# Windowed attention and a gated convolution on one core: the window as a band matmul ahead of the scores, and 25 of the loads of q and k by GpSimd's queue

## The chip, the cores and the metric

One core of a Trainium2 chip runs the whole program. TensorE (PE in the profile) multiplies matrices, VectorE (DVE), ScalarE (ACT) and GpSimd (POOL) work on elements, SyncE (SP) issues most of the DMAs. Each engine takes its own instructions strictly in the order of its own list; a semaphore wait holds the instruction that carries it and everything behind it on that engine. The metric is the device time of one execution in microseconds (us), the median over several runs.

## The reference, cut to what matters

Batch 8, 8 heads, 576 positions, 64 features to a head; then a feed-forward part with d_model 512 and d_ff 1024. Random fp32 inputs; the band, the convolution and the gate are:

```python
scores = scale * np.matmul(q, k.transpose(0, 1, 3, 2))
mask = np.abs(pos[:, None] - pos[None, :]) <= 32
scores = np.where(mask, scores, -1000000000.0)
...softmax over the keys...
x = np.matmul(attn, v)            # heads side by side: (batch, 576, 512)
h = np.maximum(x @ w_in, 0.0)
conv_out[s] = sum_k conv_w[k] * h[s - 1 + k]        # 3 taps, a weight for each of the 1024 features
out = (h * sigmoid(conv_out)) @ w_out
```

## The kernel before, in words

Everything is unrolled, and one text, `ORDER`, sets the order of the steps on all engines: each word is a step with its arguments, steps are issued in the order of the words, and every instruction is kept in that order on its engine. The digit behind an @ is the PSUM bank. A step whose data another engine or a DMA makes waits for it, and a step that reuses a buffer waits for the last reader of the buffer's old content; these waits follow from the order of the words.

Attention runs over units (b, G): a batch and a group of four heads. For each unit:

- `lq`, `lk` load 128 x 1152 fp32 of q or k (576 KB) into one of six staging tiles `st`, issued by SP; with a third argument after b and G they load half of it. `cq`, `ck` cast them to bf16 into one of the tiles `qb` (ending p: GpSimd, a: ScalarE). `tq`, `tk` transpose them on VectorE into `qT`, `kT`.
- `sc` computes the scores of four heads for one part of the positions (h = 0: four tiles of 64 queries, h = 1: five): per tile and half of the features, four matmuls with 32 rows of weights each, one for each head. `ex` takes the exponential on ScalarE into a tile `attn`. `mk` sets what lies outside the window to zero: on VectorE a product with a 0/1 tile `mask`, on GpSimd two affine selects.
- `lv` loads one of five chunks of v (192 or 256 KB) on SP, `cv` and `vo` cast and shift it (`ve`, `vo`), `av` multiplies with `attn`, `nr` divides by the row sums into `xn`; `xp` and `xe` transpose through TensorE and ScalarE, `xt` by a DMA.

The feed-forward part runs over pieces P (four halves of 192 columns, then ten of 384) and four pairs of feature blocks m2: `ph` multiplies by w_in (eight matmuls), `re` is the ReLU into `hT`, `pc` and `tp` are the three convolution taps, `th` the tanh, `ga` the gate into `gT`, `py` the product with w_out, `ye` and `st` copy and store the result. The taps have forms: P by six matmuls with 128 x 128 diagonal weights for a pair of blocks, D and A by twelve matmuls of 64 x 64, X by ScalarE and VectorE, G by GpSimd.

Weights are loaded and cast in four quarters each (`li`, `ci`, `lo`, `co`). While no data is there yet, TensorE runs products with the identity (`id,n`: n products of the identity itself; `ia,y,G,half,n`: n products that read the half of the cast tile `qb` of unit (0, G), y = 0 for q and 1 for k; nothing uses their results). A tile of `qb` is chosen by `slot(y, b, G) % NQB`, with `slot = 2 * (2 * b + G) + y`.

Of the kernel before, what the change touches and what calls it, by code (L numbers as in the profile page):

```python
# [13 lines left out]

ORDER = """
lk,0,0,0 lq,0,0,0 s3 s1 lq,0,0,1 lk,0,1,1 s2 lk,0,1,0 lk,0,0,1 cw@5 id,7@7 lq,0,1,1 lq,0,1,0 cc lv,0,2 dg,1,a dg,0,d
lv,0,1 dg,2,d cq,0,0,0,a ia,0,0,0,1@7 cq,0,0,1,p ia,0,0,1,2@7 dg,7,a ck,0,1,1,p ia,1,1,1,2@7 dg,4,a s4 tq,0,0,1 dg,5,a
tk,0,1,1 ck,0,0,0,p ia,1,0,0,6@7 dg,3,a s5 tq,0,0,0 s0 ck,0,1,0,a s7 tk,0,0,0 lv,0,3 ck,0,0,1,p ia,1,0,1,2@7 tk,0,0,1
cq,0,1,1,a tk,0,1,0 sc,0,0,1@4 tq,0,1,1 cq,0,1,0,p sc,0,0,0@0 ex,0,0,1 lv,0,4 tq,0,1,0 cv,0,2,p lv,0,0 ex,0,0,0
mk,0,0,1,d sc,0,1,1@4 id,4@3 lk,1,0 ex,0,1,1 cv,0,1,p li,1 vo,0,1,d li,3 sc,0,1,0@4 id,9@3 mk,0,0,0,d lq,1,0 cv,0,3,a  # L20
li,0 mk,0,1,1,d li,2 cv,0,4,a vo,0,2,d vo,0,3,d cv,0,0,a lq,1,1 ex,0,1,0 vo,0,0,d lk,1,1 av,0,0,0@0 mk,0,1,0,d lv,1,2
ck,1,0,a nr,0,0,0 av,0,1,0@3 id,1@7 nr,0,1,0 av,0,0,1@0 ci,1,a xp,0,1@6 nr,0,0,1 dg,6,a xp,0,0@2 xe,0,1,a ci,3,p
av,0,1,1@4 id,4@7 xe,0,0,a nr,0,1,1 ph,0,3@3 lv,1,1 cq,1,0,p tk,1,0 xp,0,2@7 re,0,3 xp,0,4@5 xp,0,3@4 xe,0,2,a
ph,0,1@0 xe,0,3,a tq,1,0 pc,0,3,P@6 ci,0,p re,0,1 ph,1,3@4 th,0,3,P xe,0,4,a ga,0,3,P sc,1,0,0@0 re,1,3 ph,0,0@5
ci,2,p ex,1,0,0 lv,1,0 pc,1,3,P@7 re,0,0 ph,2,0@4 mk,1,0,0,d th,1,3,P cq,1,1,p sc,1,0,1@0 ph,2,2@5 ex,1,0,1 ph,2,3@6
tq,1,1 re,2,2 ck,1,1,p lv,1,4 ph,2,1@3 ga,1,3,P ph,1,0@5 re,2,1 lv,1,3 tk,1,1 cv,1,2,p re,2,0 ph,1,1@0 re,1,0 re,1,1
mk,1,0,1,d lo,1 sc,1,1,0@1 cv,1,1,p lo,2 pc,0,1,P@5 ex,1,1,0 ph,0,2@7 cv,1,0,p vo,1,1,d re,2,3 sc,1,1,1@0 re,0,2
ph,1,2@4 vo,1,0,d ex,1,1,1 mk,1,1,0,d lv,2,1 av,1,0,0@6 lo,0 re,1,2 nr,1,0,0 cv,1,3,p av,1,1,0@0 lk,2,1 cv,1,4,a
pc,1,0,P@2 lo,3 nr,1,1,0 pc,1,2,P@4 vo,1,3,p th,1,0,P lv,2,0 pc,0,0,P@7 th,0,1,P ga,1,0,P th,1,2,P xp,1,0@3 mk,1,1,1,d
xp,1,1@6 co,1,p xe,1,0,a pc,1,1,P@1 lq,2,1 xe,1,1,a ga,1,2,P pc,0,2,P@2 lk,2,0 ga,0,1,P pc,2,0,X@0 ph,3,2@3 vo,1,2,p  # L30
th,1,1,P tp,2,0,X ph,3,0@4 re,3,2 th,0,2,P ph,3,1@6 re,3,0 lv,2,2 pc,3,2,G ga,0,2,P pc,2,3,P@5 th,0,0,P ga,1,1,P
re,3,1 av,1,0,1@3 co,0,a ga,0,0,P av,1,1,1@1 nr,1,0,1 pc,2,2,P@6 lq,2,0 co,2,a pc,2,1,P@7 ck,2,1,p nr,1,1,1 lv,2,3
ph,3,3@3 th,2,0,X th,2,3,P pc,3,0,P@4 re,3,3 co,3,p ga,2,3,P xp,1,4@1 th,2,1,P xp,1,3@2 pc,3,1,P@3 th,3,0,P ga,2,1,P
cv,2,0,p pc,3,3,P@5 xe,1,4,a ga,2,0,X th,2,2,P xp,1,2@1 cv,2,1,p th,3,1,P py,0,1@7 ga,2,2,P vo,2,0,p ga,3,1,P cq,2,1,a
s6 tk,2,1 lv,2,4 py,0,2@6 tp,3,2,G xe,1,2,a tq,2,1 th,3,3,P xe,1,3,a lq,3,0 ga,3,0,P lk,3,0 sc,2,1,0@0 ga,3,3,P
ck,2,0,p py,1,0@4 ex,2,1,0 ye,0,1,d cv,2,2,p th,3,2,G@5 lk,3,1 tk,2,0 ye,0,2,a vo,2,1,p sc,2,1,1@0 lv,3,0 cq,2,0,a
ga,3,2,G ph,4,3@6 ye,1,0,d ex,2,1,1 lv,3,1 tq,2,0 cv,2,3,p py,0,0@4 vo,2,2,p re,4,3 mk,2,1,0,d lk,4,0 cv,2,4,a
mk,2,1,1,d sc,2,0,1@0 ye,0,0,a vo,2,3,p av,2,1,0@6 ex,2,0,1 ph,4,2@4 nr,2,1,0 st,0,0 mk,2,0,1,d sc,2,0,0@0 cq,3,0,p
re,4,2 av,2,1,1@6 lq,3,1 st,0,1 ck,3,0,a nr,2,1,1 ph,4,1@4 pc,4,3,G ex,2,0,0 tk,3,0 av,2,0,1@6 re,4,1 ph,4,0@0
mk,2,0,0,d ck,3,1,a nr,2,0,1 av,2,0,0@4 re,4,0 pc,4,1,A@2 nr,2,0,0 xp,2,2@6 th,4,1,A pc,4,2,P@0 tq,3,0 tp,4,3,G  # L40
pc,4,0,P@4 th,4,2,P ga,4,1,A lv,3,2 py,1,2@7 xt,2,3 xt,2,1 th,4,0,P ga,4,2,P cv,3,0,a ga,4,0,P xe,2,2,a xt,2,0
sc,3,0,0@0 tk,3,1 cq,3,1,p py,1,1@6 th,4,3,G@4 st,0,2 ex,3,0,0 ga,4,3,G lq,4,0 st,1,0 cv,3,1,a mk,3,0,0,p sc,3,0,1@0
lq,4,1 ye,1,1,d py,2,0@4 lv,3,3 ex,3,0,1 tq,3,1 st,1,1 lv,3,4 ck,4,0,a mk,3,0,1,d sc,3,1,0@0 cv,3,2,p ph,5,2@5
ex,3,1,0 ye,1,2,d xt,2,4 vo,3,1,d ye,2,0,a sc,3,1,1@0 vo,3,0,d re,5,2 py,2,1@4 mk,3,1,0,d ex,3,1,1 pc,5,2,G tk,4,0
cq,4,0,a av,3,0,0@0 av,3,1,0@6 lq,5,0 ph,5,0@2 nr,3,0,0 cq,4,1,a nr,3,1,0 py,2,2@5 re,5,0 tq,4,0 xt,3,0 cv,3,3,a
ye,2,1,a mk,3,1,1,d vo,3,2,p sc,4,0,0@0 xt,3,1 ye,2,2,a pc,5,0,D@6 ex,4,0,0 ph,5,1@4 tq,4,1 lk,4,1 th,5,0,D cv,3,4,p
# [659 lines left out]
```

## Time and profile before

| | us |
|---|---|
| median of three runs | 212.5 (211.89 to 212.92) |
| the profiled execution, its own time | 212.45 |
| its span, first to last instruction | 210.7 |
| around the span | 1.75 |
| TensorE busy | 195.7 (93% of the span) |
| VectorE busy | 178.4 (85%) |
| ScalarE busy | 172.7 (82%) |
| GpSimd busy | 147.7 (70%) |
| 16 DMA engines, share of SP's queue | 84.0% |

The mean granted TensorE clock is 0.992 of full speed. Busy times overlap; what matters at any place is which engine or transfer is waited for there.

### The profile page before, as it was taken

What the parts mean: (1) busy time and instruction counts of PE and PEld (TensorE: products, weight loads), DVE (VectorE), ACT (ScalarE), POOL (GpSimd) and SP (SyncE); (2) the same over time, 40 slices, a digit from 0 to 9 for tenths busy, and PEclk for the clock granted to TensorE, in tenths of its full rate; (3) what the DMA queues carried; (4) which work ended last, traced back from release to release, by engine and by line L of the source; (5) the groups of instructions that cost most, each with busy time, mean ns of one, the idle gap of its engine ahead of it and who ended that gap; (6) DMA issues with size and microseconds to landing.
All of it is one profiled execution on the core that took longest, in us unless ns stands there. A gap on an engine that the chain in (4) does not pass through costs nothing.

```text
span 210.7 us, 7141 instructions
## 1 busy us (share of the span) xinstructions
PE 195.7 (93%) x2951; PEld 113.9 (54%) x2974; DVE 178.4 (85%) x297; ACT 172.7 (82%) x265; POOL 147.7 (70%) x177
## 2 busy tenths in 40 slices
PE   3867999999999799999999999999999999999994
PEld 2233798895465345654464554554545565555443
DVE  4677977999999998797999779899999587899860
ACT  2986798997999798779999699899978799759911
POOL 2650586499999469999699998539954879955700
PEclk9979999999999999999999999999999999999999
DMA  5999999999998895899999999999976444222225
GB/s 176 325 213 347 388 220 273 366 296 272 318 279 194 195 319 151 267 292 238 241 258 176 226 252 231 262 297 245 290 144 165 99 142 128 46 71 103 100 100 199
DMA packets 66165, 46.90 MB, mean 223 GB/s; under 512 B 53180, under 2 KB 55508, under 8 KB 66132
## 3 DMA queue, kind: packets, MB, share of 16 engines
q1 hardware_dynamic: 66096, 46.43, 84.0%
q8 instruction: 23, 0.38, 0.8%
q14 instruction: 10, 0.08, 0.1%
q10 hardware_dynamic: 36, 0.01, 0.1%
HBM read 32.52 MB, written 9.44 MB: 199 GB/s over the span
## 4 chain that ended last, share of the span: by engine, by line
PE 56%; DVE 16%; DMA 8%; SPq 7%; ACT 6%; issue 5%; ACTq 0%; DVEq 0%
PE PS L165 56%; SPq L165 7%; DVE gT L165 6%; DMA vst<-in_v_dram 6%; DVE xn L165 4%; DVE PS L165 2%; DMA st<-in_q_dram 2%; ACT hT L165 2%; ACT attn L165 1%; ACT PS L165 1%; DVE attn L165 1%; DVE rec L165 1%; ACT y L165 1%; DVE qT L165 1%; DVE kT L165 1%
## 5 line engine op out<-in xcount | busy, mean ns | idle before, releaser
L165 PE MATMUL PS<-xT,w_in_sb 128*128 128x385 bf16 (+3 forms) x448 | 69.5, 305 | 0.5 <-ACT y L165 0.3
L165 PE MATMUL PS<-w_out_sb,gT 128*128 128x512 bf16 (+1 forms) x273 | 64.7, 373 | 1.5 <-issue 0.5
L165 DVE SCALAR_TENSOR_TENSOR gT<-PS,hT 128x384 bf16<-128x384 f32 (+2 forms) x82 | 52.5, 649 | 3.9 <-ACT PS L165 2.9
L165 PEld LDWEIGHTS <-w_in_sb 128*128 128x128 bf16 x448 | 40.6, 98 | 23.1 <-issue 3.2
L165 ACT ACTIVATE hT<-PS 128x770 bf16<-128x770 f32 (+3 forms) x56 | 39.9, 722 | 9.7 <-PE PS L165 7.2
L165 PEld LDWEIGHTS <-gT 128*128 128x128 bf16 x296 | 27.6, 98 | 30.2 <-issue 1.2
L165 ACT ACTIVATE attn<-PS 128x1280 bf16<-128x1280 f32 (+1 forms) x32 | 36.0, 1132 | 4.9 <-PE PS L165 4.5
L165 POOL TENSOR_TENSOR zg<-zg,tap 128x768 f32<-128x768 f32 (+1 forms) x18 | 31.8, 1766 | 1.5
L165 ACT ACTIVATE PS<-PS 128x768 f32<-128x768 f32 (+1 forms) x47 | 29.9, 651 | 3.3 <-PE PS L165 1.9
L165 PE MATMUL PS<-hT,diag_w 64*64 64x384 bf16 (+2 forms) x354 | 27.6, 310 | 0.4 <-ACT hT L165 0.2
L165 DVE TENSOR_TENSOR xn<-PS,rec 128x512 bf16<-128x512 f32 (+1 forms) x32 | 26.4, 825 | 1.1
L165 POOL TENSOR_SCALAR ve<-vst 128x512 bf16<-128x512 f32 x24 | 16.9, 715 | 13.3 <-DMA vst<-in_v_dram 12.8
L165 POOL TENSOR_SCALAR vo<-vst 64x512 bf16<-64x512 f32 x32 | 22.7, 709 | 2.5
L165 DVE TENSOR_TENSOR attn<-attn,mask 128x1280 bf16<-128x1280 bf16 (+1 forms) x24 | 22.5, 942 | 2.2 <-ACT attn L165 2.1
L165 POOL TENSOR_SCALAR qb<-st 128x1152 bf16<-128x1152 f32 (+1 forms) x18 | 18.7, 1043 | 7.4 <-DMA st<-in_q_dram 5.4
L165 POOL TENSOR_SCALAR_AFFINE_SELECT attn<-attn 64x1024 bf16<-64x1024 bf16 (+1 forms) x16 | 19.7, 1233 | 5.3 <-ACT attn L165 4.3
L165 DVE STREAM_TRANSPOSE qT<-qb 128x576 uint32<-128x576 uint32 (+1 forms) x18 | 20.1, 1128 | 3.0 <-POOL qb L165 1.6
L165 DVE STREAM_TRANSPOSE kT<-qb 128x576 uint32<-128x576 uint32 (+1 forms) x18 | 19.9, 1123 | 1.4 <-PE PS L165 0.8
L165 POOL TENSOR_SCALAR tap<-hT,conv_w_sb 128x384 f32<-128x384 bf16 (+1 forms) x36 | 20.1, 571 | 0.9
L165 ACT COPY y<-PS 128x512 f32<-128x512 f32 (+1 forms) x24 | 13.5, 577 | 7.8 <-PE PS L165 7.7
L165 ACT CAST qb<-st 128x1152 bf16<-128x1152 f32 (+1 forms) x18 | 19.1, 1074 | 0.2 <-DVE y L165 0.2
L165 PEld LDWEIGHTS <-diag_w 64*64 64x64 bf16 (+1 forms) x354 | 15.2, 103 | 7.3 <-issue 3.4
(50 smaller groups left out, 205.6 us busy)
## 6 DMA issues: line engine op xcount, KB each, us to landing
...
st<-in_k_dram SPq DMA_DIRECT2D x14, 576.0 KB, 6.8
st<-in_q_dram SPq DMA_DIRECT2D x14, 576.0 KB, 6.1
...
```

The costliest lines, as they stand in the source:

```text
L165: return lambda *args, **kwargs: tc.keep_in_program_order(do(*args, **kwargs))
```

## The change

Five things change together:

1. The mask steps `mk` are gone. `sc` starts with eight matmuls of 32 rows (four heads, two halves of 32 columns) that write 0 inside the window and -131072 outside it into the PSUM banks; the score matmuls accumulate on top, and the exponential makes these entries zero. A tile `band` of 128 x 256 takes the place of the two mask tiles.
2. 25 of the 32 loads of q and k are steps `gq`, `gk`: a DMA issued from GpSimd's queue that reads the fp32 rows and writes bf16 straight into `qb`; for them the staging tile and the cast fall away. The four of the first batch and three later ones stay on SP with a cast. The loads of the first batch are whole instead of halves.
3. `qb` has five tiles instead of four.
4. `ORDER` is new throughout. The forms of the taps are shared out anew: of the 56 pairs, before 14 half and 5 full ones had form P, 20 D or A, 1 half and 7 full X, 1 half and 8 full G; now 12 half P, 21 D or A, 1 half and 10 full X, 3 half and 9 full G. `xp` runs 10 times instead of 11. The idle products are 10 of `id` and 20 of `ia`, before 25 and 13.
5. `ye`, `vo`, `cv` go to other engines in places (`vo` on VectorE 14 instead of 8 steps, on GpSimd 10 instead of 16). The functions `gi` and `go` are added but not used.

```diff
 ORDER = """
-lk,0,0,0 lq,0,0,0 s3 s1 lq,0,0,1 lk,0,1,1 s2 lk,0,1,0 lk,0,0,1 cw@5 id,7@7 lq,0,1,1 lq,0,1,0 cc lv,0,2 dg,1,a dg,0,d
...
+s1 cw@6 cc dg,5,d lq,0,0 s4 cq,0,0,1,a tq,0,0,1 cq,0,0,0,a dg,4,d dg,2,d lk,0,0 ck,0,0,1,p tk,0,0,1 tq,0,0,0 lv,0,0
+lv,0,1 lv,0,2 ck,0,0,0,a tk,0,0,0 s3 s2 s0 cv,0,0,a cv,0,1,a vo,0,0,d s5 lk,0,1 lq,0,1 lv,0,3 lv,0,4 dg,7,a dg,6,a
+cv,0,2,p li,0 gq,1,1 id,5@7 ia,0,0,1,1@7 ia,0,0,0,3@7 ia,1,0,1,6@7 sc,0,0,0@4 sc,0,0,1@0 ex,0,0,0 vo,0,1,d dg,3,a
+av,0,0,0@6 ck,0,1,1,a ex,0,0,1 ck,0,1,0,p tk,0,1,0 nr,0,0,0 li,1 tk,0,1,1 cq,0,1,1,p cq,0,1,0,a li,3 li,2 tq,0,1,1
+tq,0,1,0 cv,0,3,a lv,1,1 dg,1,a gk,1,1 id,3@5 ia,1,1,1,6@5 ia,0,1,1,1@5 ia,0,1,0,3@5 sc,0,1,0@0 vo,0,2,d sc,0,1,1@4
...
-    NST, NQB, NQT, NAT, NY = 6, 4, 3, 4, 4
+    NST, NQB, NQT, NAT, NY = 6, 5, 3, 4, 4
...
+    def fetch_qk(y, b, G):
+        gpsimd.dma_start(qb_[slot(y, b, G) % NQB], rows(y, b, G, ()))
...
         t0 = tiles_of(h)[0]
-        for t in tiles_of(h):
+        ts = tiles_of(h)
+        out4 = PS[:, bank:bank + 4, 0:64 * len(ts)].rearrange("p a (t x) -> p a t x", x=64)
+        for i in range(2):
+            for a in range(4):
+                lo = 32 * a
+                tensor.matmul(
+                    out4[:, a, :, 32 * i:32 * i + 32],
+                    band[lo:lo + 32, lo - 32 * i + 32:lo - 32 * i + 160],
+                    ident[lo:lo + 32, None, lo:lo + 32].broadcast_to([32, len(ts), 32]),
+                    start=(i == 0), stop=False, skip_group_check=True,
+                )
+        for t in ts:
             for e in range(2):
                 for a in range(4):
                     tensor.matmul(
                         PS[:, bank + a, 64 * (t - t0):64 * (t - t0) + 64],
                         kT[32 * a:32 * a + 32, 64 * t:64 * t + 128, e],
                         qT[32 * a:32 * a + 32, 64 * t:64 * t + 64, e],
-                        start=(e == 0), stop=(e == 1),
+                        start=False, stop=(e == 1), skip_group_check=True,
                     )
...
-    def mk(b, G, h, e):
-        attn, n = attn_of(b, G, h)
-        if e == "d":
-            vector.tensor_tensor(out=attn, in0=attn, in1=mask[:, 0:4 * n], op=ALU.mult)
-            return
-        for lo, sign in ((0, 1), (64, -1)):
-            part = attn[lo:lo + 64].rearrange("p (t x) -> p t x", x=64)
-            gpsimd.affine_select(
...
     def s2():
-        for base, sign in ((0, 1), (64, -1)):
+        for base, sign in ((-32, 1), (96, -1)):
             gpsimd.affine_select(
-                out=mask1, in_=mask1, compare_op=ALU.is_ge, fill=0.0, base=base,
-                pattern=[[-sign, 64]], channel_multiplier=sign,
+                out=band, in_=band, compare_op=ALU.is_ge, fill=MASKED, base=base,
+                pattern=[[sign, 256]], channel_multiplier=-sign,
             )
```

Three places of the new lists are shown, with the waits of each instruction in brackets: a name such as DMAHW2 stands for a DMA issued by SP or ScalarE, DMASW0 and DMASW1 for the first and the second DMA issued by GpSimd, an engine's name for an instruction of that engine. A number behind a tile's name is the buffer (qb1 is the second of the tiles `qb`) and a running number.

TensorE at the start of the program, before: the idle products that read k's tile (qb1), and the first scores behind them.

```order
L165 LDWEIGHTS ident0_113
L165 MATMUL PS_118<-qb1_68,ident0_113 128x512 [waits Pool_49]
...
L165 LDWEIGHTS kT0_74 [waits DVE_49]
L165 MATMUL PS_118<-qT0_71,kT0_74 128x64
```

The same place now:

```order
L161 MATMUL PS_118<-qb0_67,ident0_114 128x512
L161 LDWEIGHTS ident0_114 [waits DMASW0_49]
L161 MATMUL PS_118<-qb1_68,ident0_114 128x512 [waits Pool_49]
...
L161 LDWEIGHTS band0_115 [waits Pool_49]
L161 MATMUL PS_118<-ident0_114,band0_115 128x4x32
...
L161 LDWEIGHTS kT0_75 [waits DVE_49]
L161 MATMUL PS_118<-qT0_72,kT0_75 128x64
```

Six products read qb1, as `ia,1,0,1,6` says. The word `gq,1,1` stands ahead of them in `ORDER`, and its slot is 6 % 5 = 1: it writes the same tile, so the products wait for its DMA (DMASW0) as well as for the cast, and the band and the first scores stand behind them.

GpSimd at the start of the program now (rows from its first work on data to its third DMA; before, the same stretch held casts and selects and no DMA):

```order
L161 TENSOR_SCALAR qb1_68<-st1_62 128x576 [waits DMAHW2_49]
L161 AFFINE_SELECT band0_115<-band0_115 128x256 [waits DVE_49]
L161 AFFINE_SELECT band0_115<-band0_115 128x256 [waits Pool_49]
L161 MEMSET vst0_78 32x512
L161 MEMSET vst0_78 32x512 [waits Pool_49]
L161 TENSOR_SCALAR ve0_79<-vst0_78 128x8x64 [waits DMAHW5_49,Pool_49]
L161 DMA qb1_68<-in_q_dram 128x1152 [waits DVE_49]
L161 TENSOR_SCALAR qb3_70<-st3_64 128x576 [waits DMAHW6_49]
L161 TENSOR_SCALAR qb2_69<-st2_63 128x576 [waits DMAHW7_49]
L161 DMA qb2_69<-in_k_dram 128x1152 [waits DVE_49,Pool_49]
```

The first DMA is `gq,1,1`; it stands behind the cast of the third chunk of v (ve0 from vst0). The second is `gk,1,1`, into slot 7 % 5 = 2, the tile of unit (0, 1)'s q; it waits for the transposes of that tile on VectorE.

TensorE ahead of the second unit's scores, now:

```order
L161 MATMUL PS_118<-qb3_70,ident0_114 128x512 [waits Activation_49]
...
L161 LDWEIGHTS ident0_114 [waits DMASW1_49]
L161 MATMUL PS_118<-qb2_69,ident0_114 128x512 [waits Pool_49]
L161 LDWEIGHTS ident0_114
L161 MATMUL PS_118<-qb2_69,ident0_114 128x512 [waits Activation_49]
...
L161 LDWEIGHTS kT1_76 [waits DVE_49]
L161 MATMUL PS_118<-qT1_73,kT1_76 128x64 [waits DVE_49]
```

Four products (`ia,0,1,1,1` and `ia,0,1,0,3`) read qb2 behind `gk,1,1` in `ORDER`, and so wait for its DMA (DMASW1); the scores of unit (0, 1) stand behind them. On ScalarE, between the first exponential and the cast that ends this tile, now:

```order
L161 ACTIVATE attn0_83<-PS_118 128x1024 [waits PE_49]
L161 ACTIVATE diag_w0_113<-ident0_114,conv_w_sb0_112 128x128 x3
L161 CAST qb3_70<-st3_64 128x576 [waits DMAHW6_49]
L161 ACTIVATE attn1_84<-PS_118 128x1280 [waits PE_49]
L161 CAST qb2_69<-st2_63 128x576 [waits DMAHW7_49]
```

Before, the casts of the first batch's q and k all stood ahead of the first exponential on ScalarE.

More of the change, by code (lines that the diff above doesn't have):

```diff
@@ L143 @@
     ident = tiles(1, [128, 128], BF16, "ident")[0]
-    mask = tiles(1, [128, 4 * 5 * 64], BF16, "mask")[0]
-    mask1 = tiles(1, [128, 64], BF16, "mask1_")[0]
+    band = tiles(1, [128, 256], BF16, "band")[0]
     conv_w24 = tiles(1, [3 * MB, 128], FP32, "conv_w24")[0]
@@ L428, in like, with conv_out @@
         return ap
-    def conv_out(P, m2):
-        return psum2(where["pc", P, m2], width(P))
+    def conv_out(P, m2, kind="P"):
+        bank = where["pc", P, m2]
+        if kind in "AD":
+            return PS[:, bank:bank + 2, 0:width(P)]
+        return psum2(bank, width(P))
     n_g = [0]
```

182 lines of the change are left out of this document (84 added, 98 removed).

## The prediction

> **What bounds the kernel now.** I read the busy times over three stretches first (columns after the stretch and its length: TensorE, its weight loads, VectorE, ScalarE, GpSimd, each with its instructions; granted TensorE clock, share of the 16 DMA engines, GB/s). The cuts are the first matmul with w_in and the last matmul of all.
>
> ```profile
> 0.00:24.30 24.30, 16.91 (x273) 8.55 (x274) 16.59 (x50) 17.37 (x33) 8.44 (x18) 0.93 0.91 280
> 24.30:207.80 183.50, 178.83 (x2680) 105.39 (x2701) 161.77 (x248) 154.99 (x232) 139.25 (x159) 1.00 0.85 216
> 207.80:210.70 2.90, 0.00 (x0) 0.00 (x0) 0.00 (x0) 0.34 (x1) 0.00 (x0) 1.00 0.39 142
> ```
>
> From 24.3 us on TensorE is busy for 178.83 of 183.50 us and all others have room: I call this the body, and it is bound by TensorE. It can only shrink by TensorE's own work or by the 4.7 us in which it idles. The first 24.3 us are something else; there the timeline of each engine counts (start, length, engine, operation, how many; in brackets the idle time before and what ended it).
>
> ```profile
> 3.74 3.03 PE L165 MATMUL PS<-ident 128*128 128x512 bf16 x7
> 8.01 2.09 PE L165 MATMUL PS<-qb,ident 128*128 128x512 bf16 x8 [0.20 <-POOL qb L165]
> 11.64 0.76 PE L165 MATMUL PS<-qT,kT 32*128 32x64 bf16 x72 [0.16 <-DVE kT L165]
> 24.30 0.83 PE L165 MATMUL PS<-xT,w_in_sb 128*128 128x193 bf16 x8
> 7.29 1.31 POOL L165 TENSOR_SCALAR qb<-st 128x576 bf16<-128x576 f32 x2 [0.38 <-DMA st<-in_k_dram]
> 12.20 3.29 ACT L165 ACTIVATE attn<-PS 128x1280 bf16<-128x1280 f32 x3 [0.59 <-PE PS L165]
> 17.57 0.62 ACT L165 CAST ve<-vst 128x512 bf16<-128x512 f32 x1 [1.57 <-DMA vst<-in_v_dram]
> 18.47 0.62 ACT L165 CAST ve<-vst 128x512 bf16<-128x512 f32 x1 [0.28 <-DMA vst<-in_v_dram]
> 19.00 1.02 ACT L165 ACTIVATE attn<-PS 128x1024 bf16<-128x1024 f32 x1
> 20.05 0.69 DVE L165 TENSOR_TENSOR attn<-attn,mask 128x1024 bf16<-128x1024 bf16 x1 [0.33 <-ACT attn L165]
> ```
>
> Scores begin at 11.64, then the chain waits for v (ScalarE's casts at 17.57 and 18.47 sat idle for its DMAs), and the last exponential of the batch, its mask, `av`, `nr` and `xp` lead to the first `ph` at 24.30. So the end is where the first `ph` starts, plus the body, plus 2.9 us.
>
> **The start, step by step.** The lists of the changed kernel show two waits that were not there. The six idle products ahead of the first scores read the tile that `gq,1,1` writes, and four ahead of the second unit's scores the tile that `gk,1,1` writes. TensorE does nothing behind them until these two DMAs have landed, though the scores need neither. Behind the first stand all scores; `gk,1,1` itself is issued only after the second unit's transposes, whose last cast stands on ScalarE behind the first two exponentials. The two DMAs thus lie one after the other in one chain. Durations by shape (busy, mean ns), and the landing times of all loads of q and k (min, median, max):
>
> ```profile
> L165 ACT ACTIVATE attn<-PS 128x1280 bf16<-128x1280 f32 x16 | 19.8, 1240 | 3.4 <-PE PS L165 3.2
> L165 ACT ACTIVATE attn<-PS 128x1024 bf16<-128x1024 f32 x16 | 16.4, 1025 | 1.5 <-PE PS L165 1.2 <-POOL ve L165 0.3
> L165 ACT ACTIVATE diag_w<-ident,conv_w_sb 128x128 bf16<-128x128 bf16 x18 | 5.6, 389 | 0.0
> L165 ACT CAST qb<-st 128x576 bf16<-128x576 f32 x3 | 1.9, 661 | 0.0
> L165 DVE STREAM_TRANSPOSE qT<-qb 128x288 uint32<-128x288 uint32 x4 | 2.7, 709 | 1.6 <-POOL qb L165 1.6
> L165 POOL TENSOR_SCALAR ve<-vst 128x512 bf16<-128x512 f32 x24 | 16.9, 715 | 13.3 <-DMA vst<-in_v_dram 12.8
> DMA to landing us min/median/max: 3.0/6.4/11.8
> st<-in_q_dram SPq DMA_DIRECT2D x14, 576.0 KB, 6.1
> ```
>
> - The first two whole tiles hold what four halves held: landed at 7.3, when GpSimd's wait for the fourth half ended. Three loads of v follow; two 192-KB loads landed 0.9 us apart (17.57 to 18.47), so 0.9 and twice 1.2 give 10.6. GpSimd's cast, two selects and two memsets before that take some 2.5 us and are covered. It then casts the third chunk, 0.7, and issues `gq,1,1` at 11.3.
> - No row shows a DMA of GpSimd's. Nearest are SP's loads of the same 576 KB. The second unit's loads stand in SP's queue beside it, so I take the median of the loads of q, 6.1; the ends are 3.0 (a load with nothing ahead) and 11.8. Landed: 17.4.
> - Six products: between 1.6 (eight in 2.09) and 2.6 (seven in 3.03, at the start); 2.1. 19.5.
> - Scores to exponential 0.56 (11.64 to 12.20) and eight band matmuls, together 0.7; the exponential 1.0. 21.2.
> - On ScalarE three diagonals (0.98 for three), a cast, the second exponential, a cast: 3.5; the last transpose 0.7. `gk,1,1` goes out at 25.4. VectorE's own queue (`nr`, three transposes) is done slightly earlier, so ScalarE decides.
> - SP's queue is emptier by then: 4.5, about midway between 3.0 and 6.1. 29.9. Four products, 1.2: 31.1.
> - From these scores to the first `ph`: 0.7 to the exponential, then what the trace shows from the exponential at 19.00 to 24.30, less the mask: 5.3 - 0.7. First `ph` at 36.4.
>
> That is **12.1 us later** than 24.3. With both landings at 3.0 and the short products it is 6.8 later (11.3 + 3.0 + 1.6 + 0.7 + 1.0 + 4.2 + 3.0 + 1.0 + 5.3 = 31.1); with 11.8, 6.4 and the slow products 20.7 later.
>
> The Trainium skill (DMA: Bandwidth & Descriptors, section on the anatomy of a DMA on the gpsimd path) prices such a DMA at about 2.0 us plus its bytes at 436 GB/s, as an estimate 3.4 us for this load. The sum above with 3.4 in both places would be 3.8 us less, and the time 215.6. The trace's loads of this size took 3.4 us only when nothing stood before them, and here SP's loads run on the same 16 engines, so I stay with the rows.
>
> **The body, TensorE's work.**
>
> ```profile
> L165 PE MATMUL PS<-hT,diag_w 64*64 64x384 bf16 x240 | 13.4, 330 | 0.0
> L165 PE MATMUL PS<-hT,diag_w 128*128 128x192 bf16 x84 | 8.7, 246 | 0.2 <-issue 0.2
> L165 PE MATMUL PS<-hT,diag_w 128*128 128x384 bf16 x30 | 5.6, 326 | 0.2 <-ACT hT L165 0.2
> L165 PE MATMUL PS<-ident,xn 128*128 128x128 bf16 x36 | 3.3, 220 | 0.1
> 29.75 0.48 PE L165 MATMUL PS<-qT,kT 32*128 32x64 bf16 x40
> 30.16 3.60 PE L165 MATMUL PS<-xT,w_in_sb 128*128 128x193 bf16 x40
> ```
>
> Five full pairs in form P go: -5.6. Two half pairs less: 8.7 / 14 = 0.62 each, -1.2. One more D: 13.4 / 20, +0.7. Four `xp` matmuls: -0.4. Against it the band. The scores' forty matmuls give way to the next after 0.41 us (29.75 to 30.16), four of them in 0.041. A stream of 193 columns takes 0.090 a matmul (3.60 / 40); at that pace four matmuls of 64 columns would take 0.12 one by one, so the four run side by side. For the band, 128 or 160 columns take 0.060 or 0.075 at that pace, and two groups of four come to 0.13 for a set of scores; 28 of 32 sets lie in the body: +3.8. Ends: 2.3 if a group costs the 0.041 of the scores whatever its columns, 15 if the eight run one by one. Sum: **-2.8**.
>
> **The body, the others.** What goes and what comes on the lighter engines lies beside TensorE and costs or brings nothing but through its 4.7 us of idle time.
>
> ```profile
> L165 DVE TENSOR_TENSOR attn<-attn,mask 128x1280 bf16<-128x1280 bf16 x13 | 13.8, 1059 | 0.3 <-ACT attn L165 0.3
> L165 DVE TENSOR_TENSOR attn<-attn,mask 128x1024 bf16<-128x1024 bf16 x11 | 8.8, 804 | 1.9 <-ACT attn L165 1.9
> L165 POOL TENSOR_SCALAR_AFFINE_SELECT attn<-attn 64x1024 bf16<-64x1024 bf16 x10 | 11.4, 1142 | 4.8 <-ACT attn L165 4.1 <-DVE gT L165 0.4
> L165 POOL TENSOR_SCALAR_AFFINE_SELECT attn<-attn 64x1280 bf16<-64x1280 bf16 x6 | 8.3, 1385 | 0.5 <-ACT attn L165 0.3
> L165 ACT CAST qb<-st 128x1152 bf16<-128x1152 f32 x15 | 17.2, 1157 | 0.2 <-DVE y L165 0.2
> L165 POOL TENSOR_SCALAR qb<-st 128x1152 bf16<-128x1152 f32 x13 | 15.4, 1186 | 2.3 <-DMA st<-in_q_dram 1.1 <-DMA st<-in_k_dram 0.9
> L165 POOL TENSOR_TENSOR zg<-zg,tap 128x768 f32<-128x768 f32 x16 | 29.8, 1862 | 1.3
> L165 POOL TENSOR_SCALAR vo<-vst 64x512 bf16<-64x512 f32 x32 | 22.7, 709 | 2.5
> L165 SPq DMA_DIRECT2D st<-in_k_dram x18: 328/555/3056, 0.8 to 146.3; - x18
> ```
>
> VectorE loses 22.6 us of masks, ScalarE 14 of its 15 whole casts (16.2). GpSimd loses 19.7 of selects, 11 of 13 whole casts (13.0) and 12 `vo` copies (8.5); it gains one full and two half pairs in form G (two additions of 1.86 and six smaller products to a full pair: some 7, and 5 for a half, 17 in all) and 25 DMA issues. Without the issues it falls from 139 to about 115 of 183.5. An issue I bound by nothing and, far off, by the cast of the same tile, 1.2; SP's own take a median of 0.56. I take 1.2, the row that is GpSimd's own work on this tile: 30 us, back to 145. SP loses 25 loads and its later loads of v, transposes and stores come forward. I let half of TensorE's idle time go, -2.4; the ends are all of it, -4.7, and 3 more when an issue stands in GpSimd's list waiting for a tile of `qb` while `cv`, `vo` and the taps of form G wait behind it.
>
> **The sum.** Span 210.7 + 12.1 - 2.8 - 2.4 = 217.6. The profiled execution's own time lies 1.75 above its span (212.45) and 0.05 from the median: **219.4 us**. From the short ends (6.8, -2.8, -4.7) it is 211.8, from the long ones (20.7, -2.8, +3) 233.4.
>
> **The rivals.**
>
> - *Short waits and a smoother body: faster.* Both DMAs land in 3.0 and TensorE's idle time goes; that leaves 211.8. What lies hidden in its busy time must give the rest: each switch from one group of matmuls to the next holds a tail, 0.07 of the 0.48 us of the row of forty scores, and where lighter engines let groups follow closely, 4 us of the body's 178.8 may go: 207.8. For it: ScalarE loses 16 of 173 us, VectorE 23 of 178 against three more pairs in form X. Against it: 3.0 is the fastest of 36 landings. It decides once the slip of the start is smaller than what the body gains by over 1.1.
> - *GpSimd or its DMAs become the bound: much slower.* GpSimd's 115 us plus 25 issues fill the body from (183.5 - 115) / 25 = 2.7 us for an issue on; at 3.2 the body is 12 us longer: 231. Against it: SP's 0.56 is far from 2.7, though nothing shows GpSimd's.
> - *The band's matmuls run one by one:* 15 in place of 3.8: 231. Against it: the scores.
> - *The slip and the gain cancel:* a slip of 5 to 6 us, just under the short end, against the 5.2 of the body: 212 to 213.
> - *The idle products don't wait:* they are no work, but the wait is in the list, so the change does do this; I give it no chance of its own beyond the first rival's.
>
> **How the numbers follow.** Forecast 0.62, faster 0.16, GpSimd's bound 0.11, cancel 0.07, one by one 0.04. A measurement of this kernel cannot tell less than about 0.5%, 1.1 us. Faster 0.16; the same 0.07; slower 0.77. The forecast's own range is 212 to 227; to hold 8 in 10 over all cases I leave a tenth out at each end, 209 to 228.
>
> **What would show it.** In the profile of the changed kernel: TensorE idle from the products on q's tile at about 8 us until about 17, ended by the landing of GpSimd's first DMA; its second idle stretch, from about 23 to 30, ended by the second; first `ph` at 36 (31 to 45); no waits on GpSimd's DMAs after that. In the body: the 256 band matmuls at 4 to 5 us in all, diagonals at 21.5 instead of 27.7, TensorE over 97% busy. The prediction is wrong if the first scores start before 14, if the first `ph` starts before 30, or if the body is longer than 184.

## The result, and the profile after

| | before | after |
|---|---|---|
| median (lowest to highest) | 212.34 us (211.89 to 212.92) | **232.61 us** (228.94 to 235.28) |
| ratio, 95% interval | 1 | 1.0853 [1.072, 1.0986] |
| profiled execution: time, span | 212.45, 210.7 | 232.05, 230.2 |
| first `ph` | 24.30 | 37.03 |
| from there to the last matmul (the body) | 183.4 | 189.3 |
| what is left of the span | 3.0 | 3.9 |

The ratios here and below are taken from the runs of each kernel that lie within 1.5% of its fastest (for the changed kernel 228.94 and 232.05 us), and the profiled executions of e1_free, e4_gq, e7_vfirst, e10_xp, e18_away and e19_thin are longer than that, so that their bodies come out too long.

Forecast were 219.4 and a range of 209 to 228. The direction is right and the size is not. Of the 19.5 us between the spans, 12.7 lie in the start (forecast 12.1), 5.9 in the body (forecast -5.2) and 0.9 behind it. The start first, in the timeline of the changed kernel's TensorE and GpSimd (start, length, engine, operation, how many; in brackets the idle time before and what ended it):

```profile
10.14 0.62 POOL L161 TENSOR_SCALAR ve<-vst 128x512 bf16<-128x512 f32 x1 [0.71 <-DMA vst<-in_v_dram]
10.71 0.73 POOL L161 DMA_DIRECT2D qb<-in_q_dram  x1
16.45 2.74 PE L161 MATMUL PS<-qb,ident 128*128 128x512 bf16 x6 [9.01 <-DMA qb<-in_q_dram]
25.45 0.59 POOL L161 DMA_DIRECT2D qb<-in_k_dram  x1 [11.74 <-DVE vo L161]
30.22 1.89 PE L161 MATMUL PS<-qb,ident 128*128 128x512 bf16 x4 [6.26 <-DMA qb<-in_k_dram]
37.03 0.83 PE L161 MATMUL PS<-xT,w_in_sb 128*128 128x193 bf16 x8
```

Both waits stand where the lists put them: TensorE is idle for 9.01 us until the load `gq,1,1` has landed and for 6.26 until `gk,1,1` has, held up by idle products; the scores behind them need neither load. The body, in the view of windows (length of the window, busy time of PE, PEld, DVE, ACT and POOL with the number of instructions, granted clock of TensorE, share of the DMA engines, GB/s) and of TensorE's waits (in total, how often, longest):

```profile
37.03:226.32 189.29, 178.75 (x2869) 106.28 (x2891) 153.01 (x250) 148.05 (x228) 120.87 (x165) 0.99 0.79 158
```

```profile
PE PS L161 <- DMA xT<-xn: 4.7, 2, 3.4
PE PS L161 <- DVE kT L161: 1.4, 1, 1.4
```

TensorE is busy as long as before (178.8 us in both), though it was to do 2.8 us less; it idles for 10.5 us in place of 4.6. All others have become lighter than before: VectorE 153 (161.8), ScalarE 148 (155.0), GpSimd 121 (139.3). In the body the longest waits are for `xT<-xn`, SP's transposes of the attention's result by DMA, which were no wait of TensorE's before. This wait is paid twice. The same view of windows around the longest:

```profile
127.03:132.03 5.00, 4.84 (x62) 2.34 (x61) 4.83 (x7) 4.29 (x7) 4.60 (x7) 1.00 1.29 152
132.03:137.03 5.00, 1.61 (x9) 0.71 (x8) 0.96 (x1) 0.85 (x2) 2.79 (x5) 0.95 1.07 201
137.03:142.03 5.00, 5.00 (x61) 2.92 (x60) 3.43 (x8) 2.42 (x3) 3.83 (x5) 0.71 1.17 243
```

TensorE waits for 3.39 us in the second row, and in the third it works all the time at 0.71 of its clock: another 1.5 us. The Trainium skill (TensorE: Matmul & The Clock Gate, Part 1: The HAM clock gate) says that the clock halves after an idle window of about 3.4 us and comes back after as long a busy one. These rows agree, but other runs lost the clock after shorter waits as well: a wait of 2.03 us in e8_both and one of 2.66 in e19_thin were each followed by 5 us at 0.66, while one of 2.35 in e5_xt was followed by 5 us at 1.00. Here the measurement decides, and a wait above 2 us may be paid twice.

The chain of waits says what the body has come to depend on (start, length, what held it):

```profile
83.30 7.73 DMA vst<-in_v_dram
103.46 5.79 DMA vst<-in_v_dram
116.61 3.46 DMA vst<-in_v_dram
128.56 6.73 DMA xT<-xn
```

Four DMAs that SP issues stand in the body's part of it, three loads of v and a transpose, 23.7 us together. Before, it held two, a load of v (6.07) and a load of q (5.02). So the question of the runs was what makes these, or something else, late.

### The profile page after: what moved, and what is told of

Read it like the earlier page. It is cut to its first block, busy times and chain, and to the rows that moved or that the text cites. A ratio compares the mean times of both kernels' runs of the same rounds, so it can differ in the third digit from the quotient of the medians.

```text
span 230.2 us, 7531 instructions
## 1 busy us (share of the span) xinstructions
PE 195.6 (85%) x3163; PEld 115.0 (50%) x3188; DVE 167.7 (73%) x295; ACT 164.2 (71%) x257; POOL 132.2 (57%) x187
## 3 DMA queue, kind: packets, MB, share of 16 engines
q0 software_dynamic: 3600, 7.37, 21.4%
## 4 chain that ended last, share of the span: by engine, by line
PE 43%; DVE 18%; DMA 18%; POOL 7%; issue 5%; ACT 4%; SPq 3%; DVEq 0%; POOLq 0%; ACTq 0%
PE PS L161 43%; DMA vst<-in_v_dram 10%; DVE gT L161 7%; DVE xn L161 6%; SPq L161 3%; DMA xT<-xn 3%; POOL zg L161 3%; DMA qb<-in_q_dram 2%; ACT attn L161 2%; DMA qb<-in_k_dram 2%; POOL tap L161 2%; DVE qT L161 1%; DVE kT L161 1%; DVE rec L161 1%; POOL vo L161 1%
## 5 line engine op out<-in xcount | busy, mean ns | idle before, releaser
L161 ACT ACTIVATE attn<-PS 128x1024 bf16<-128x1024 f32 (+1 forms) x32 | 36.1, 1131 | 22.0 <-PE PS L161 20.7
L161 PEld LDWEIGHTS <-gT 128*128 128x128 bf16 x296 | 27.7, 98 | 31.4 <-issue 1.8
L161 POOL TENSOR_TENSOR zg<-zg,tap 128x768 f32<-128x768 f32 (+1 forms) x24 | 38.6, 1609 | 2.0
L161 POOL TENSOR_SCALAR zg<-hT,conv_w_sb 128x384 f32<-128x384 bf16 (+1 forms) x24 | 13.1, 554 | 39.0 <-ACT hT L161 39.0
L161 POOL TENSOR_SCALAR tap<-hT,conv_w_sb 128x384 f32<-128x384 bf16 (+1 forms) x48 | 25.9, 551 | 0.9
L161 DVE RECIPROCAL rec<-PS 128x8 f32<-128x8 f32 (+1 forms) x32 | 6.7, 209 | 26.7 <-PE PS L161 26.1
L161 DVE SCALAR_TENSOR_TENSOR PS<-hT,conv_w_sb,PS 128x384 f32<-128x384 bf16 (+1 forms) x44 | 23.4, 598 | 0.8 <-ACT PS L161 0.6
L161 PE MATMUL PS<-hT,diag_w 64*64 64x384 bf16 (+1 forms) x324 | 21.5, 318 | 0.1
L161 PE MATMUL PS<-qb,ident 128*128 128x512 bf16 x19 | 7.4, 531 | 15.6 <-DMA qb<-in_q_dram 9.0
L161 DVE COPY vo<-ve 64x520 bf16<-64x520 bf16 x28 | 11.0, 391 | 8.6 <-POOL ve L161 7.9
L161 PE MATMUL PS<-qT,kT 32*128 32x64 bf16 x1152 | 15.3, 194 | 1.4 <-DVE kT L161 1.4
```

The source lines that it names most:

```text
L161: return lambda *args, **kwargs: tc.keep_in_program_order(do(*args, **kwargs))
```

## The experiments

All changes are to words of `ORDER` unless said. For each run the table has the ratio to the kernel before with its 95% interval, and from the profiled execution the first `ph`, the body and TensorE's busy time in it, from a row of the view of windows as quoted above. A dash stands where the profile isn't used. Some records of TensorE are missing: the traces of before, after and e9_old to e19_thin hold only some 255 of the 280 widest products with w_out, those of e1_free to e8_both all of them. That is about 2 us of busy time (these products come to 62.9 us in before and 65.0 in e3_band), so busy times are best compared within one of the two groups.

| run | ratio | first `ph` | body | PE busy |
|---|---|---|---|---|
| after | 1.085 [1.072, 1.099] | 37.03 | 189.3 | 178.8 |
| e1_free | 1.039 [1.033, 1.046] | 25.07 | 195.7 | 184.8 |
| e2_hw | 1.112 [1.105, 1.120] | 22.80 | 206.2 | 184.9 |
| e3_band | 1.007 [1.001, 1.012] | 22.11 | 185.7 | 183.5 |
| e4_gq | scattered, see there | 26.32 | 189.8 | 182.1 |
| e5_xt | 1.026 [1.018, 1.033] | 22.47 | 187.7 | 179.3 |
| e6_tiles | 1.046 [1.039, 1.054] | 22.48 | 192.6 | 181.6 |
| e7_vfirst | median 224.94 us | - | - | - |
| e8_both | 1.065 [1.057, 1.072] | 22.65 | 195.2 | 182.6 |
| e9_old | 1.074 [1.066, 1.081] | 27.79 | 192.3 | 184.3 |
| e10_xp | 1.039 [1.029, 1.049] | 25.12 | 192.5 | 180.7 |
| e11_sp | 1.037 [1.029, 1.044] | 22.17 | 190.6 | 180.2 |
| e12_noband | 1.037 [1.028, 1.047] | 22.11 | 191.0 | 176.9 |
| e14_noqk | 1.001 [0.997, 1.006] | 21.28 | 183.1 | 177.3 |
| e15_nov | 1.045 [1.038, 1.053] | 22.58 | 192.7 | 179.9 |
| e16_noload | 1.008 [1.003, 1.013] | 21.39 | 184.5 | 177.1 |
| e17_bandx | 1.107 [1.097, 1.117] | 23.77 | 205.9 | 181.9 |
| e18_away | 1.037 [1.029, 1.045] | 22.64 | 192.6 | 180.0 |
| e19_thin | 1.011 [1.006, 1.016] | 23.49 | 186.7 | 178.6 |

### The parts of the change one by one

**e1_free**, the two waits of the start taken away:

```diff
-li,0 gq,1,1 id,5@7 ia,0,0,1,1@7 ia,0,0,0,3@7 ia,1,0,1,6@7 sc,0,0,0@4
+li,0 id,5@7 ia,0,0,1,1@7 ia,0,0,0,3@7 ia,1,0,1,6@7 gq,1,1 sc,0,0,0@4
-gk,1,1 id,3@5 ia,1,1,1,6@5 ia,0,1,1,1@5 ia,0,1,0,3@5 sc,0,1,0@0
+id,3@5 ia,1,1,1,6@5 ia,0,1,1,1@5 ia,0,1,0,3@5 gk,1,1 sc,0,1,0@0
```

> The changed kernel with two words moved: gq,1,1 and gk,1,1 stand behind the idle products that read their tiles, so these products wait for the casts alone; every engine keeps its order. Theory (the two waits make the slip of the start): the first matmul with w_in, at 37.0 in the changed kernel, comes back to 21 to 25 us, the rest from there stays at 193 us, and the span falls from 230 to 215 to 218. Rival (the stretch from 80 to 140 us is limited by DMA traffic that starts with the program and not with TensorE): the start comes back, but the rest grows by as much, and the span stays above 224.

The ratio falls from 1.085 to 1.039, which is some 10 us (between the medians it is 12.6, 232.61 to 219.99), and the first `ph` comes 12.0 us earlier. The two waits make the slip of the start. What is left, 3.9%, lies nearly all in the body.

**e2_hw**, e1_free with the 25 loads back on SP, at the same places, cast right ahead of their transposes:

```diff
-gq,2,1 ... tq,2,1
+lq,2,1 ... cq,2,1,p tq,2,1
```

> As e1_free, and the 25 loads of GpSimd's queue are SP's again, at the same places of the order, with a cast on GpSimd or ScalarE in turn right ahead of each transpose. Theory (GpSimd's loads hold up the loads of v and the DMA transposes by sharing the DMA engines): the waits for transposes and for v in the middle shrink, and the stretch behind the first matmul with w_in is 4 us or more shorter than in e1_free. Rival (the new order of SP's list and of the forms makes those waits): it is as long as in e1_free or longer, by the 25 casts of 1.15 us on two engines that have room, 0 to 6 us.

The highest ratio of all: at these places a load on SP with a cast on GpSimd or ScalarE behind it, right ahead of the transpose, is dearer than the load by GpSimd without one. How much of that is the queue and how much the cast, this run doesn't tell.

**e3_band**, the kernel before with the band and without masks:

```diff
-ex,2,1,0 ... mk,2,1,0,d
+ex,2,1,0
```

> The kernel before with the band matmuls and no mask steps, all else as it was. Theory (the band costs TensorE 0.13 to 0.15 us a set of scores, 4 to 5 us in all, and the masks lay beside TensorE): 1 to 4 us slower than before. Rival (masks were on the way to the products, so that taking them off gives back more than the band costs): 1 to 5 us faster. Rival (each change to rows of 32 and back costs more than the matmuls): over 8 us slower.

The first `ph` comes 2.2 us earlier and the body is 2.3 longer; the band pays for itself and no more.

**e4_gq**, the kernel before with the 25 loads by GpSimd into five tiles, each where its tile comes free, masks kept:

```diff
-lq,2,1 ... cq,2,1,a tq,2,1
+gq,2,1 ... tq,2,1
```

> The kernel before with the same 25 loads by GpSimd's queue and without their casts, each put where its tile of qb comes free, five tiles; masks and order as before. Theory (in the changed kernel GpSimd's queue used 21.4% of 16 engines for 230.2 us, 1.97 us a load, against about 1.6 that SP's queue lost per load, so DMA time grows by some 9 us where it is already short): 2 to 8 us slower than before. Rival (casts of 29 us off ScalarE and GpSimd and a queue of their own for q and k help): 1 to 5 us faster.

216.24, 221.00, 222.75 and 255.59 us: too scattered for a ratio. In the profiled one (221.0) the body is 6.4 us longer than before, though 25 casts of ScalarE and GpSimd are gone. The shortest of the four is 4.8 us below it, so that much of the 6.4 may be scatter.

**e9_old**, e3_band and e4_gq together, both ingredients in the old order:

> The order of before with both ingredients: band ahead of the scores and no masks (as e3_band, 1.007), and the 25 loads by GpSimd without casts, each placed where its tile comes free (as e4_gq, about 1.02 to 1.05 with a large scatter). Theory ingredients (GpSimd's late loads into five tiles cost the body its time in any order): 1.02 to 1.05. Theory new order (the loads are harmless, and what hurts is how the new order lays SP's and GpSimd's lists): 1.00 to 1.015.

Neither theory's number: 1.074. Of 12.4 us that its span has over e3_band's, 5.7 are a start in which `w_in` comes later (the first `ph` waits 5.62 us for its cast), and 6.5 are body. So with GpSimd's loads the body is 6.5 us longer in the old order too, and the new order is not needed for the loss; e4_gq, with masks, points the same way with less certainty. Whether the loads do it by coming late or by being in the way, these two runs don't tell.

### Is q or k late, is SP's list in the way, is it TensorE's work?

**e5_xt**, e1_free with one transpose moved out of the way of three loads of v:

```diff
-tp,2,1,X xt,1,2 pc,3,2,P@0 ... lv,2,0 ... lv,2,4 ... lv,2,3 th,3,0,P
+tp,2,1,X pc,3,2,P@0 ... lv,2,0 ... lv,2,4 ... lv,2,3 xt,1,2 th,3,0,P
```

> As e1_free (the changed kernel with its two early GpSimd loads behind the idle products; ratio 1.039, body some 193 us), but SP's word xt,1,2, a transposing load that waits nine microseconds for xn while lv,2,0 lv,2,4 lv,2,3 stand behind it, goes behind these three. Theory SP-line (in the new order SP's list puts loads of v behind words that wait for the computation): the dip of DMA traffic at 40 to 50 us fills, the v loads of the second batch issue from 41 us on in place of 51, and the body gets 3 to 6 us shorter: ratio 1.010 to 1.025. Theory tile-lookahead (five tiles for q and k hold GpSimd's loads back): nothing changes, 1.035 to 1.045.

1.026, at the edge of what theory SP-line gave: the blocked line had been worth about 3 us (the intervals of e1_free and e5_xt just touch). What followed from that theory did not hold:

**e7_vfirst** (25 loads of v, from the third batch on, ahead of transposes and stores) and **e11_sp** (eight words chosen from the trace; the diff shows three of its moves):

```diff
-st,0,2 ... xt,2,1 ... lv,3,3 ... lv,3,4 ... st,2,0 ... xt,3,1
+st,0,2 ... lv,3,3 lv,3,4 xt,2,1 ... xt,3,1 st,2,0
```

> As e5_xt, and in the whole order from the third batch on each v load (25 of 30 words move) stands at most ten words behind the last copy that reads its chunk of the batch before, ahead of the transposes and stores of SP that stood before it. Theory SP-line: SP's waits no longer delay v, the chain loses its DMA steps on vst, and the body falls by 5 to 9 us against e1_free: ratio 0.995 to 1.015. Theory tile-lookahead: 1.03 to 1.045. Third way: SP now waits for the copies in front of transposes and stores, which come later in their turn, and the time rises above 1.045.

> As e5_xt, with eight words of SP's list in other places and nothing else: lv,3,3 lv,3,4 ahead of xt,2,1; st,2,0 (a store that waits 4.6 us for ScalarE's copy) behind xt,3,1; xt,4,4 and st,3,1 behind xt,4,0; lv,6,1 ahead of xt,5,0; lv,6,4 ahead of vd,6,0 (waits 6.6 us). Theory SP-line: the body gets 2 to 4 us shorter, ratio 1.007 to 1.018. Theory other: 1.022 to 1.03.

e7_vfirst took 220.27 us at the least, more than e5_xt's longest run (217.80), and e11_sp has 1.037. These other places in SP's list bring nothing more.

**e6_tiles**, e1_free with nine tiles and loads four slots ahead, and **e8_both**:

```diff
-NST, NQB, NQT, NAT, NY = 6, 5, 3, 4, 4
+NST, NQB, NQT, NAT, NY = 4, 9, 3, 4, 4
```

(e8_both is e6_tiles and e7_vfirst together.)

> As e1_free, but nine bf16 tiles for q and k in place of five (paid for by two fp32 staging tiles fewer), and each GpSimd load from the third batch on moved to the place in the order of the load four slots ahead of it, where its tile is free in the new count. Theory tile-lookahead: q and k land 10 us and more ahead of their transposes, the DMA dip at 40 to 60 us fills, and the body falls by 5 us or more: ratio 1.00 to 1.02. Theory SP-line: v and xn's transposes stay late, so ratio 1.03 to 1.045.

> e6_tiles and e7_vfirst together. If the body's six microseconds are late loads of either kind, both theories give the shortest time of the four: ratio 0.99 to 1.01, with TensorE over 97% busy in the body. If it stays above 1.03, late loads are not the cause, and the new order itself (which engine does what, and when) is.

In e6_tiles every GpSimd load from the third batch on is issued 17 us or more ahead of its transpose; the timelines of GpSimd and VectorE show one of them:

```profile
96.73 1.14 POOL L162 DMA_DIRECT2D qb<-in_k_dram  x2
...
142.93 1.24 DVE L162 STREAM_TRANSPOSE kT<-qb 128x576 uint32<-128x576 uint32 x1
```

The first of the two loads at 96.73 is read at 142.93. The time does not fall, if anything it rises (1.046), and with both kinds of loads early, in e8_both, it is 1.065. Nor does VectorE wait for these loads where they come later: in e5_xt its transposes of q and k stand idle for 0.9 us in all until a load by GpSimd has landed. Late q and k are not the cause; theory tile-lookahead has fallen. (The nine tiles were paid for with two staging tiles; what that costs was not tried apart.)

**e12_noband**, e5_xt without the band's 256 products:

```diff
-        for i in range(2):
-            for a in range(4): ... band ...
+        (nothing; the scores' first matmul has start=(e == 0))
```

> As e5_xt without the 256 band products, so that the scores stay unmasked (this part of the computation is left out). If TensorE's work sets the body, the time falls by at least the 4 us that the band adds to it: ratio 1.005 or less. If the body is set by the chain through SP's list, xn and GpSimd, TensorE has spare time and the ratio stays at 1.015 or more.

TensorE has 256 products fewer, and the time is no shorter. (Its busy time, 176.9 us after 179.3 in e5_xt, doesn't measure this: 1.6 of the 2.4 us are records that its trace lacks, and its clock in the body is lower, 0.98 after 1.00.) In the new order the body isn't bound by TensorE's work, the term I worked out most closely.

**e10_xp**, e5_xt with the four transposes for which TensorE waited done by TensorE:

```diff
-xt,3,0 pc,5,0,X@6 xt,3,1 sc,4,0,0@0 ... ex,4,0,0
+xp,3,0@5 xe,3,0,a pc,5,0,X@6 sc,4,0,0@0 ... ex,4,0,0 xp,3,1@5 xe,3,1,a
```

> As e5_xt (ratio 1.026), but four transposes of xn, xt,3,0 xt,3,1 xt,4,1 xt,4,0, for whose landing TensorE waited 1.53 and 2.35 us there, are done by TensorE in a free bank and evicted by ScalarE: 16 products of 0.22 us and 4 copies more, four DMA transposes of 1.3 us of SP fewer. Theory transposes (SP's transposing loads land too late, 5 to 7 us after their xn): the two waits go and what follows comes earlier, ratio 1.005 to 1.018. Theory other: the 3.5 us of TensorE work eat the gain, the waits move elsewhere, 1.023 to 1.04.

1.039: no gain. Taking these four transposes of thirty off the DMA engines is no remedy.

### Which loads, and by what

**e14_noqk**, **e15_nov** and **e16_noload** take the loads from the third batch on out of e5_xt: q and k, v, both.

```diff
-gq,2,1 ... lq,2,0 ... ck,2,1,p ... gk,2,0 ...      (e14_noqk, e16_noload)
-lv,2,0 ... lv,2,4 ... lv,2,3 ...                    (e15_nov, e16_noload)
```

> As e5_xt without any load or cast of q and k from the third batch on (that part of the computation is left out: later batches use what lies in the tiles): 22 GpSimd loads, 3 SP loads and 4 casts fewer. If q and k by GpSimd are what the body waits for (their landing, their 0.6 us each on GpSimd's list, or their traffic), the body falls by 5 us or more: ratio 1.00 or less. If it waits for v and the transposes of xn, 1.015 to 1.03.

> As e5_xt without the 30 loads of v from the third batch on (left out; the copies of v stay). If v behind SP's waits sets the body, the body falls by 5 us or more: ratio 1.00 or less. If the loads of v are not it, 1.015 to 1.03.

> e14_noqk and e15_nov together: no load from the third batch on, only transposes of xn and stores. If late loads of either kind make the body 6 us longer, the ratio is 0.99 or less. If it stays above 1.01, no load is to blame, and the new order of the engines' lists itself (with the transposes of xn on SP) does not run as fast as it was laid out.

(In e14_noqk 21 GpSimd loads and three casts are gone, one fewer of each than its expectation counts.) That settles which: without q and k the ratio is 1.001, without v it is 1.045, above e5_xt. Without either it is 1.008, no better than without q and k alone. The views of DMA issues of before, after, e5_xt and e14_noqk, in this order (how many, median us from issue to landing), and of TensorE's waits in e5_xt point to what they hit:

```profile
xT<-xn SPq DMA_TRANSPOSE x29, 3.8
```

```profile
xT<-xn SPq DMA_TRANSPOSE x30, 3.7
```

```profile
xT<-xn SPq DMA_TRANSPOSE x30, 4.2
```

```profile
xT<-xn SPq DMA_TRANSPOSE x30, 2.5
```

```profile
PE PS L161 <- DMA xT<-xn: 4.0, 3, 2.4
```

Without these loads of q and k the transposes land in 2.5 us in place of 4.2, TensorE waits for none of them in place of 4.0 us, and the body is 4.6 us shorter. The changed kernel itself has 3.7, no more than before (3.8): its transposes didn't land later than before, but TensorE now waits for them. e15_nov tells the same from the other side; its timelines of SP, GpSimd and TensorE:

```profile
114.14 3.85 SPq L159 DMA_TRANSPOSE xT<-xn  x3
...
113.65 0.61 POOL L159 DMA_DIRECT2D qb<-in_q_dram  x1
117.31 0.61 POOL L159 DMA_DIRECT2D qb<-in_k_dram  x1
...
124.58 2.73 PE L159 MATMUL PS<-xT,w_in_sb 128*128 128x385 bf16 x8 [4.42 <-issue]
```

SP issues the last three transposes of the fifth batch from 114.14 on, the third at 116.7, and GpSimd two loads at 113.65 and 117.31. The last transpose lands 7.8 us after its issue, and the `ph` that reads it starts at 124.58, after 4.42 us of idle time. No load of v is under way in this stretch, only GpSimd's loads and four stores by SP.

**e19_thin** keeps GpSimd's instructions and takes nearly all bytes away (e5_xt otherwise):

```diff
-        gpsimd.dma_start(qb_[slot(y, b, G) % NQB], rows(y, b, G, ()))
+        to, src = qb_[slot(y, b, G) % NQB], (q, k)[y][b, 4 * G:4 * G + 4, :, :]
+        n = D if b >= 2 else RP * D
+        gpsimd.dma_start(to[:, 0:n], bass.AP(src.tensor, src.offset, [[RP * D, 128], [1, n]]))
```

> As e5_xt (ratio 1.026; transposes of xn land 4.16 us after their issue in the median, 2.50 in e14_noqk), but each GpSimd load from the third batch on fetches one of its 18 rows a partition, 16 KB written in place of 288 (the rest of the tiles is stale: that part of the computation is left out). The same 25 instructions, waits and descriptors on GpSimd's list, hardly any traffic. Theory traffic (the bytes stand in the DMA engines ahead of xn's transposes, for which TensorE waits): median landing of the transposes 2.5 to 3.0 us, ratio 0.995 to 1.010, near e14_noqk. Theory list (what costs is GpSimd's 0.6 us for each and its waits for a free tile): 1.018 to 1.03, transposes that land in 2.5 us all the same. Theory lateness of q and k themselves: also near 1.00, but e6_tiles with its leads of 17 us and more speaks against it.

1.011, just above the range of theory traffic and well below that of theory list. Its view of DMA issues:

```profile
xT<-xn SPq DMA_TRANSPOSE x30, 3.0
```

TensorE waits for no transpose here. The issue and landing of each transpose tell the same. In e5_xt, 14 were issued while a load by GpSimd was under way and landed in 4.7 us in the median, 13 others in 3.7. In e19_thin, with hardly any bytes, it is 2.6 (8 of them) against 3.0. So of the 2.6% of e5_xt about 1.5, give or take 0.9, are bytes. The 1.0 that e14_noqk gains beyond it (GpSimd's instructions and waits, three loads of SP, three casts) I didn't split.

**e18_away**, nine tiles as in e6_tiles, and nine loads (the expectation says ten) moved to keep clear of the transposes that TensorE had waited for:

```diff
-gk,5,1 st,2,1 tp,5,2,G
+st,2,1 tp,5,2,G gk,5,1
-pc,7,1,G ... gq,7,0 ... tp,7,1,G ... gk,7,0
+gq,7,0 pc,7,1,G ... tp,7,1,G ... vo,5,0,p gk,7,0
```

> Nine tiles for q and k as in e6_tiles on the order of e5_xt, so that the loads are free to move, and ten of GpSimd's loads moved by a few words so that none is issued in the 5 us ahead of or amid the transposes xt,3,0 xt,3,1 and xt,4,1 xt,4,4 xt,4,0, for which TensorE waited (gk,5,1 behind them; gq,7,0 4 us earlier and gk,7,0 4 us later; gk,4,1 gq,4,1 gk,6,1 gk,6,0 earlier; gq,6,0 later). All bytes are loaded. Theory traffic: these transposes land within 3 us of their issue, the waits on them go, ratio 1.00 to 1.018 against 1.046 of e6_tiles. Theory list or order: 1.025 to 1.045.

A miss in time, 1.037, but a close view of what happens to single transposes. The chain of waits of e5_xt, of the transposes alone, and that of e18_away:

```profile
80.06 6.66 DMA xT<-xn
115.29 5.30 DMA xT<-xn
```

```profile
69.33 8.28 DMA xT<-xn
...
123.07 2.47 DMA xT<-xn
```

The transpose `xt,4,0` (115.29 in e5_xt, 123.07 here), from whose way two loads were moved, now lands in 2.47 us in place of 5.30. An earlier one has taken its place in the chain with 8.28. The timeline of GpSimd shows what stands beside it:

```profile
69.32 0.60 POOL L161 DMA_DIRECT2D qb<-in_k_dram  x1
69.93 0.54 POOL L161 DMA_DIRECT2D qb<-in_q_dram  x1
```

Two of GpSimd's loads go out in the same microsecond as that transpose (69.33). The second, `gq,5,0`, is one of the moved: in e6_tiles it stood five words earlier, here right behind `gk,5,0`. SP's own traffic is there too, a store at 68.05 and loads of v from 70.66 on, so that the 8.28 us are not GpSimd's alone. One collision was taken away and another came: the bytes have to go somewhere among thirty transposes.

**e17_bandx**, a try at a faster kernel: e3_band with the five full convolution pieces of TensorE shared as X pieces:

```diff
-pc,4,2,P@0 ... th,4,2,P ... ga,4,2,P
+pc,4,2,X@0 tp,4,2,X ... th,4,2,X ... ga,4,2,X
```

> As e3_band (the order of before with the band and no masks: 1.007, TensorE work 183.5 us and only 5.2 us idle), but the five convolution pieces that TensorE does in full after the first batch (4,2 4,0 6,0 10,0 10,2) are shared as the X pieces are, one tap by ScalarE and two by VectorE. VectorE has been freed of 22 us of masks there. If TensorE sets that kernel's body, five times some 1.6 us go: ratio 0.97 to 0.99, faster than both kernels. If VectorE's or ScalarE's lists set it, 1.00 or more.

1.107: my expectation fell. TensorE's diagonal products shrink from 27.2 to 22.6 us, but it idles for 24 us of a body that is 20 longer. Each piece puts four products into VectorE's list and two activations into ScalarE's, at places laid without them. TensorE's waits name VectorE first, 9.3 us for `gT` and 7.1 for `xn`; whether ScalarE stands behind these was not pursued. No kernel of the study beats the one before; e3_band comes nearest with all of the computation.

## Why the prediction was right or wrong, point by point

- **The start: right, to 0.6 us.** 12.7 us in place of 12.1, by the steps of the forecast: issue at 10.71 (forecast 11.3), landing 5.7 later (6.1), second issue at 25.45 (25.4), landing 4.7 later (4.5), first `ph` at 37.03 (36.4). The hit is a little closer than its steps: issue and landing of the first load came 1.0 us sooner than forecast together, and the two groups of idle products took 2.7 and 1.8 us where 2.1 and 1.2 were put. e1_free shows the cause: two words moved, and the first `ph` is 12.0 us earlier. The prices from SP's loads (the median, 6.1, and 4.5) held. By the formula of the Trainium skill (DMA: Bandwidth & Descriptors, section on the anatomy of a DMA on the gpsimd path), as an estimate 3.4 us for each, the two landings would have been 3.6 us too short together.
- **TensorE's work: the rows right, the sum not.** The diagonals came to 21.5 us (27.7 before; the forecast's three terms make -6.1). The band goes as priced, four side by side, so the rival with eight matmuls one by one is out. The timeline of e5_xt:

```profile
114.70 0.29 PE L161 MATMUL PS<-ident,band 32*128 32x128 bf16 x8
114.82 0.41 PE L161 MATMUL PS<-qT,kT 32*128 32x64 bf16 x32
```

  Eight matmuls give way to the scores after 0.12 us, where 0.12 was priced for 128 columns. But of the -2.8 only -1.6 shows in the busy time of e14_noqk (177.3 after 178.8), which has the same products and a clock of 1.00 in the body, and -0.1 in the changed kernel, whose clock there is 0.99. And e12_noband shows that this term no longer decides the time.
- **The step that failed: "The body, the others", -2.4.** I let half of TensorE's 4.7 us of idle time go, because all other engines become lighter and "SP loses 25 loads and its later loads of v, transposes and stores come forward". They became lighter, and TensorE's idle time rose by 5.9 us in place of falling by 2.4; some of it was paid again in clock. The body is 5.9 us longer where -5.2 was forecast, and its 189.3 us lie above the 184 that I had named as the sign of being wrong; TensorE is busy for 94% of it, not 97. What I counted was engine time. What the runs show in its place, above the kernel before: 1.3% for a transpose that stood ahead of three loads of v in SP's list (e1_free to e5_xt), about 1.5% for the bytes of GpSimd's loads, which delay the transposes that TensorE now waits for (e5_xt to e19_thin), and 1.0% not split (e19_thin to e14_noqk). The far end of the term (+3, for an issue that waits in GpSimd's list) can have a part in that last 1.0% only, some 2 us.
- **The rivals:** an issue by GpSimd takes 0.53 to 0.73 us, where I took 1.2. The rival with GpSimd as the bound, decided from 2.7 us, is out as priced: GpSimd is busy for 121 of 189 us. That its 231 us lie near the measured time is chance. Its other half, "or its DMAs", is what happened, but I had priced it by GpSimd's time and not by whom its bytes delay. The two rivals with a short slip, and the one in which the idle products don't wait, are out by the slip of 12.7 us and its two waits.
- **The Trainium skill** (DMA: Bandwidth & Descriptors, Issuing engines are not separate DMA queues) says that the DMAs of all engines run on the same 16 DMA engines and interleave, so that another issuing engine saves only the time of issuing. I had used that for the landing of GpSimd's loads and not for what these loads do to SP's. The 8.28 us of a transpose beside two such loads and SP's own agree with it.
- **Open:** the kernel before moves the same q and k, and its transposes take 3.8 us as well; yet TensorE waits for none there. That one list on SP keeps loads and transposes apart in a planned order, and that its `ph` stand further behind its transposes, is argued and not shown. Open too is why e15_nov is above e5_xt. And even without any load of q, k and v from the third batch on, the new order's body (184.5) is no shorter than the old one's (183.4), so that freeing the DMA engines does not bring the 5 us that I forecast as a gain.
